# Retention followed by a gated feed-forward: one attention step moved and reordered, and three PSUM bank assignments changed

## Chip, cores, metric

The kernel runs on one core of a Trainium2 chip. The metric is the device time of one execution in microseconds (us). The span of a profiled execution, from its first to its last instruction, is shorter than the time reported for that same execution (308.8 against 310.72 for the kernel before); positions below count from the start of the span.

## Reference

```python
# attention without softmax: 8 batches, 8 heads, 576 positions, head dim 64
scores = q @ k.T / sqrt(64)
ret = scores * D          # D[h,i,j] = gamma_h ** (i-j) for i >= j, else 0
x = (ret @ v)             # -> (8*576, 512)
# feed-forward on 4608 tokens: w_in 512x2048, w_out 2048x512
h = x @ w_in
g = h * cos(h)
out = g @ w_out
```

All arrays are fp32 outside; the kernel multiplies in bf16.

## The kernel before

The engines go by the profile's names: TensorE (PE) multiplies matrices and writes to PSUM, a memory in banks from which VectorE (DVE) and ScalarE (ACT) read; GpSimd (POOL) prepares q, k and v; SyncE (SP) issues most of the DMAs, which load the inputs, store the output and, from group 8 on, transpose q and k into `qkT`.

Tokens are handled in 36 groups of 128. Attention of a group needs its scores (L173), a masked copy `ret` made by VectorE (L182), a running state (L201) and its masked copy `sb`, and an output (L230, L243) that is cast to `xT` (L255). The feed-forward takes tiles of 512, 256, 256 and then 512 tokens: `mm1` makes `h` in blocks of two PSUM banks (L270), ScalarE makes its cosine (L278), VectorE the product `gT` (L279), and `mm2` multiplies by w_out (L287). The order of all instructions is set by hand: attention steps of later groups are sown between the matmuls of earlier tiles.

PSUM has five tags, each with one buffer: `a`, `b`, `m` (two banks each), `n` and `st` (one each). A new use of a tag waits until the last reader of the old use has finished.

```python
def transposes(g, banks=None, only=(0, 1)):
    if g >= N_PE_T:                      # from group 8 on: by DMA
        nc.sync.dma_start(qkT, qks..., transpose=True)
        return
    for m in only:                       # groups below 8: on TensorE
        ps = psum.tile(..., tag=banks[m])
        ...                              # 4 transposes, then ScalarE copies ps to qkT

def scores(g, bank, idle=0):
    ps = psum.tile([P, 2, HG, P], F32, tag=bank)
    ...                                  # 8 matmuls qkT -> ps        (L173)
    nc.vector.tensor_tensor(out=ret, in0=ps, in1=mask)              # (L182)

def attn_out(gs, bank, evac=nc.vector.tensor_copy):
    ps = psum.tile([P, len(gs), HG, P], F32, tag=bank)
    ...                                  # sb x qT (L230), ret x vb (L243)
    evac(xT of these tokens, ps)                                    # (L255)

def mm1(n, et, c0, w, bank, inside={}):
    ps = psum.tile([P, 1024 // w, w], F32, tag=bank)
    for j in range(1024 // w):
        if j in inside: inside[j]()      # attention steps sown into a block
        ...                              # 4 matmuls                  (L270)
    # ScalarE: cos, VectorE: gT = ps * cos
# ... cut ...
banks = {0: "abmabmab", 1: "amba", 2: "bmab", 3: "mamabmab"}.get(n, "abmabmab")
inside = {
    (0, 0): {3: lambda: (state(3), attn_out([3], "m"))},
    (1, 0): {4: lambda: scores(5, "b")},
    (1, 1): {3: lambda: attn_out([5], "b", evac=nc.scalar.copy)},
}
# todo: (index of the mm2 matmul before which the step stands, step)
elif n == 2:
    todo = pair(g, "ab", 11, 24) + pair(g + 2, "ba", 31, 40)[:2]   # scores of 10 in b, of 11 in a
    late += [lambda: (state(g + 3), attn_out([g + 2, g + 3], "b"))]   # after block (3,1)
elif n + 1 < len(widths):
    todo = [ ...
        (25 if n == 3 else 20, lambda: (attn_out([g, g + 1], "m"), scores2(g + 2))),
        (52, lambda: (attn_out([g + 2, g + 3], "m"), scores2(g + 4))),   # in tile 3: scores of 16, 17
        ... ]
```

(The code is abridged; "..." stands for what is left out.) "Block (n,i)" below is block i of `mm1` in tile n, both counted from 0.

## Time and profile before

| | kernel before |
|---|---|
| time, first three runs | 312.71, 312.77, 312.76 us |
| span of the profiled execution | 308.8 us |
| TensorE (PE) busy | 302.1 us, 98% |
| TensorE weight loads | 171.2 us, 55% |
| VectorE (DVE), ScalarE (ACT) busy | 176.1 us, 116.7 us |

The page of the profile has the busy time by engine, and rows of 40 equal slices of the span (here 7.7 us each) in tenths:

```profile
PE 302.1 (98%) x2361; PEld 171.2 (55%) x2361; DVE 176.1 (57%) x179; ACT 116.7 (38%) x136; POOL 97.2 (31%) x120
...
PE   8899999999999999999999999999999999999996
...
DMA  8999999999999999999990999279935510110012
...
PE 72%; DMA 11%; SPq 11%; POOL 3%; issue 1%; ACT 1%; DVE 0%; POOLq 0%; ACTq 0%
```

PE is the bound. The last line is the chain of work that ended last: 72% of it is PE, but 22% of the span is DMA and the DMA-issuing queue (SPq). The DMA row says why: the 16 DMA engines are at 90% and more for the first half of the span.

A busy share of 98% does not say where PE waited, so its timeline is read at the places that the change touches. Columns: start, duration, engine, line, what, count, and in brackets the idle time before with what ended it. First PE from 17.5 to 22 us:

```profile
17.82 1.48 PE L270 MATMUL h<-xT,w_in_sb 128*128 128x256 bf16 x12
19.14 0.39 PE L201 MATMUL st<-vb,qks 128*128 128x128 bf16 x4
19.37 0.39 PE L230 MATMUL ov<-qT_112,sb 128*128 128x128 bf16 x4
19.68 0.41 PE L243 MATMUL ov<-ret,vb 128*64 128x128 bf16 x8
20.03 0.61 PE L270 MATMUL h<-xT,w_in_sb 128*128 128x256 bf16 x4
20.91 1.36 PE L270 MATMUL h<-xT,w_in_sb 128*128 128x256 bf16 x11 [0.27 <-DVE xT L255]
```

The same stretch on ScalarE:

```profile
18.09 0.62 ACT L158 CAST vb<-fv 128x512 bf16<-128x512 f32 x1 [1.33 <-DMA fv<-in_v_dram]
18.62 0.58 ACT L255 CAST xT<-ov 128x512 bf16<-128x512 f32 x1
```

Block (0,1) starts at 20.91, when the fourth group's `xT` is there. The ends of matmuls are modelled, so the idle time of 0.27 is too small: by starts (the distance between the starts of two matmuls, less the usual distance), the gap before it is 0.542 us where 0.109 is usual for 256 columns, a stall of 0.43.

Then PE around the start of the second tile, and from 84 to 88 us, and from 116.5 to 118.5 us:

```profile
49.28 0.38 PE L287 MATMUL o<-w_out_sb,gT 128*128 128x512 bf16 x1
49.73 1.05 PE L270 MATMUL h<-xT,w_in_sb 128*128 128x128 bf16 x16
...
84.08 0.62 PE L173 MATMUL sc<-qkT 64*128 64x128 bf16 x16
84.63 0.39 PE L287 MATMUL o<-w_out_sb,gT 128*128 128x512 bf16 x1
84.86 1.91 PE L270 MATMUL h<-xT,w_in_sb 128*128 128x256 bf16 x16
86.93 1.14 PE L270 MATMUL h<-xT,w_in_sb 128*128 128x256 bf16 x9 [0.16 <-DVE ret L182]
...
116.60 0.40 PE L173 MATMUL sc<-qkT 64*128 64x128 bf16 x8
117.30 0.40 PE L173 MATMUL sc<-qkT 64*128 64x128 bf16 x8 [0.31 <-DMA qkT<-qks]
```

From 49.28 to 49.73 are 0.446 us where a matmul of 512 columns takes 0.216: a stall of 0.23 that shows no bracket. At 86.93 PE waits for bank a (0.32 by starts), at 117.30 for the DMA that transposes qkT of group 17 (0.47 by starts).

### The profile page before, as it was taken

Reading aid. Unit: us, or ns where it says so; the run is one execution under the profiler, and the core shown is the slowest. Engines: PE = TensorE matmul, PEld = TensorE weight load, DVE = VectorE, ACT = ScalarE, POOL = GpSimd, SP = SyncE. Lnnn points to the kernel's source line nnn. Section 1 sums busy time; section 2 is a strip of 40 time slices with the busy share of each in tenths; the row PEclk is TensorE's granted clock in tenths of the full one; section 3 lists DMA queues with packets and bytes.
Section 4 is the critical chain, followed back from the end, with each engine's and each line's share of the span. In section 5 each row is a group of like instructions: output and inputs, shape, how many; then the busy total and the mean of one; then the engine's idle time right before and its main releaser. Section 6 shows DMA issues by size and latency. Waiting matters only on the chain.

```text
span 308.8 us, 5686 instructions
## 1 busy us (share of the span) xinstructions
PE 302.1 (98%) x2361; PEld 171.2 (55%) x2361; DVE 176.1 (57%) x179; ACT 116.7 (38%) x136; POOL 97.2 (31%) x120
## 2 busy tenths in 40 slices
PE   8899999999999999999999999999999999999996
PEld 3478547857588554445544554455445544554444
DVE  5766424565777764755466556755576556724610
ACT  3566234615046212640264016511551056015611
POOL 2740066644563554452542244214430000000000
PEclk9999999999999999999999999999999999999999
DMA  8999999999999999999990999279935510110012
GB/s 212 210 210 207 202 227 217 213 225 209 196 235 203 234 219 218 227 196 198 239 244 3 213 214 228 28 166 227 232 59 70 136 37 0 36 68 34 2 65 71
DMA packets 148697, 49.65 MB, mean 161 GB/s; under 512 B 138688, under 2 KB 144192, under 8 KB 148672
## 3 DMA queue, kind: packets, MB, share of 16 engines
q1 hardware_dynamic: 144448, 45.10, 77.3%
q0 software_dynamic: 4224, 4.19, 8.2%
q8 instruction: 18, 0.29, 0.4%
q14 instruction: 7, 0.06, 0.1%
HBM read 36.70 MB, written 9.44 MB: 149 GB/s over the span
## 4 chain that ended last, share of the span: by engine, by line
PE 72%; DMA 11%; SPq 11%; POOL 3%; issue 1%; ACT 1%; DVE 0%; POOLq 0%; ACTq 0%
PE o L287 33%; PE h L270 31%; SPq L107 8%; DMA fq<-in_q_dram 5%; DMA fk<-in_k_dram 5%; PE ov L243 2%; PE sc L173 2%; PE st L201 2%; SPq L146 2%; PE ov L230 1%; DMA qkT<-qks 1%; POOL qks L133 1%; POOL qks L132 1%; SPq L298 1%; PE tr L151 0%
## 5 line engine op out<-in xcount | busy, mean ns | idle before, releaser
L287 PE MATMUL o<-w_out_sb,gT 128*128 128x512 bf16 (+2 forms) x608 | 134.8, 368 | 0.3 <-DVE ret L182 0.3
L270 PE MATMUL h<-xT,w_in_sb 128*128 128x512 bf16 (+2 forms) x832 | 127.6, 313 | 0.6 <-DVE xT L255 0.3
L279 DVE TENSOR_TENSOR gT<-h,cosh 128x1024 bf16<-128x1024 f32 x72 | 88.2, 1225 | 56.7 <-ACT cosh L278 56.6
L270 PEld LDWEIGHTS <-w_in_sb 128*128 128x128 bf16 x832 | 75.7, 98 | 51.2 <-issue 1.5
L278 ACT ACTIVATE cosh<-h,half_pi 128x1024 f32<-128x1024 f32 x72 | 80.2, 1113 | 52.1 <-PE h L270 52.1
L287 PEld LDWEIGHTS <-gT 128*128 128x128 bf16 x608 | 55.3, 98 | 56.8 <-issue 0.6
L132 POOL TENSOR_TENSOR qks<-fq,gq 128x512 bf16<-128x512 f32 x32 | 33.3, 1042 | 107.9 <-DMA fq<-in_q_dram 103.0
L296 ACT COPY ot<-o 128x512 f32<-128x512 f32 (+2 forms) x38 | 21.4, 563 | 120.6 <-PE o L287 117.6
L133 POOL TENSOR_TENSOR qks<-fk,gk 128x512 bf16<-128x512 f32 x35 | 36.5, 1042 | 13.5 <-DMA fk<-in_k_dram 12.2
L182 DVE TENSOR_TENSOR ret<-sc,tri 128x1024 bf16<-128x1024 f32 x32 | 38.0, 1218 | 3.6 <-PE sc L173 3.6
L210 DVE TENSOR_TENSOR sb<-st,diag_105 128x512 bf16<-128x512 f32 x32 | 22.0, 687 | 28.9 <-PE st L201 28.9
L255 DVE CAST xT<-ov 128x1024 bf16<-128x1024 f32 (+1 forms) x17 | 19.7, 1161 | 24.3 <-PE ov L243 24.3
L139 POOL CAST vb<-fv 128x512 bf16<-128x512 f32 x32 | 19.5, 610 | 7.8 <-DMA fv<-in_v_dram 5.9
L201 PEld LDWEIGHTS <-qks 128*128 128x128 bf16 (+1 forms) x128 | 9.3, 97 | 7.5 <-issue 1.3
L201 PE MATMUL st<-vb,qks 128*128 128x128 bf16 (+1 forms) x128 | 12.4, 219 | 0.1
L243 PE MATMUL ov<-ret,vb 128*64 128x128 bf16 x288 | 12.0, 222 | 0.0
L173 PEld LDWEIGHTS <-qkT 64*128 64x128 bf16 x288 | 8.1, 94 | 5.8 <-ACT qkT L156 2.3
L173 PE MATMUL sc<-qkT 64*128 64x128 bf16 x256 | 10.3, 217 | 0.3 <-DMA qkT<-qks 0.3
L230 PEld LDWEIGHTS <-sb 128*128 128x128 bf16 x128 | 8.3, 98 | 3.7
L156 ACT COPY qkT<-tr 128x512 bf16<-128x512 bf16 x12 | 6.6, 587 | 9.0 <-PE tr L151 9.0
L243 PEld LDWEIGHTS <-vb 128*64 128x64 bf16 x288 | 8.7, 109 | 2.0
L230 PE MATMUL ov<-qkT,sb 128*128 128x128 bf16 (+1 forms) x116 | 8.8, 215 | 0.0
(45 smaller groups left out, 53.5 us busy)
## 6 DMA issues: line engine op xcount, KB each, us to landing
out_dram<-ot SPq DMA_DIRECT2D x35, 256.0 KB, 4.1
fk<-in_k_dram SPq DMA_DIRECT2D x32, 256.0 KB, 4.9
fv<-in_v_dram SPq DMA_DIRECT2D x32, 256.0 KB, 4.9
fq<-in_q_dram SPq DMA_DIRECT2D x28, 256.0 KB, 4.1
w_in_sb<-in_moe_w_in_dram POOLq DMA_DIRECT2D x4, 512.0 KB, 8.9
w_out_sb<-in_moe_w_out_dram POOLq DMA_DIRECT2D x4, 512.0 KB, 16.1
fq_110<-in_q_dram SPq DMA_DIRECT2D x2, 512.0 KB, 4.4
fq<-in_q_dram SPq DMA_DIRECT2D x8, 128.0 KB, 4.1
```

The lines of the kernel that those rows point to most:

```text
L107: i = nc.sync.dma_start(f[p0:p1], src[b, :, s0 : s0 + p1 - p0, :].rearrange("h s d -> s h d"))
L132: nc.gpsimd.tensor_tensor(out=qks[:, 0], in0=fq, in1=tq, op=ALU.mult)
L133: (nc.vector if g == 3 else nc.gpsimd).tensor_tensor(out=qks[:, 1], in0=fk, in1=tk, op=ALU.mult)
L173: nc.tensor.matmul(ps[:, he, hg, :], lhsT=qkT[d0 : d0 + D, HG + hg, :], rhs=qT[d0 : d0 + D, hg, :], start=True, stop=True,)
L182: nc.vector.tensor_tensor(out=ret.rearrange("p a b i -> p (a b) i"), in0=ps.rearrange("p a b i -> p (a b) i"), in1=mask.unsqueeze(1).to_br ...
L201: nc.tensor.matmul(ps[:, hg, :], lhsT=qks[p0:, 1, 2 * hg : 2 * hg + 2, :].rearrange("s h d -> s (h d)"), rhs=vb[p0:, 2 * hg : 2 * hg + 2, ...
L210: nc.vector.tensor_tensor(out=sb, in0=ps, in1=diag2.unsqueeze(1).to_broadcast([P, HG, P]), op=ALU.mult,)
L243: nc.tensor.matmul(ps[he * D : he * D + D, x, hg, :], lhsT=vb[:, 2 * hg + he, :], rhs=ret[:, he, hg, :], start=(g % PER == 0 and hg == 0), ...
L270: nc.tensor.matmul(ps[:, j, :], lhsT=w_in_sb[:, dg, (et + j) * P : (et + j + 1) * P], rhs=xT[:, dg, c0 : c0 + w], start=(dg == 0), stop=(d ...
L278: nc.scalar.activation(cosh, ps, ACTF.Sin, bias=half_pi, scale=1.0)
L279: nc.vector.tensor_mul(gT[:, et : et + m, c0 : c0 + w], ps, cosh)
L287: nc.tensor.matmul(ps, lhsT=gT[:, et, tsi * P : (tsi + 1) * P], rhs=w_out_sb[:, et, c0:c1], start=(et == 0), stop=(et == ET - 1),)
```

## The change

Its intent is to take PE's small stalls away. (1) The fourth group's output is issued before its state update and one step (4 matmuls) sooner, so that `xT` is ready when block (0,1) wants it. (2) Block (1,0) takes bank b instead of a, which ScalarE is still copying from. (3) To make room, scores and output of group 5 move to bank a; block (1,2) keeps b. (4) The scores of groups 10 and 11 swap banks, so that block (3,1), in a, follows the first `ret` and not the second. No instruction is added or removed.

```diff
-            vb = tiles.pop(("a", g))[1]
+            vb = tiles["a", g][1]
...
-        banks = {0: "abmabmab", 1: "amba", 2: "bmab", 3: "mamabmab"}.get(n, "abmabmab")
+        banks = {0: "abmabmab", 1: "bmba", 2: "bmab", 3: "mamabmab"}.get(n, "abmabmab")
...
-                (0, 0): {3: lambda: (state(3), attn_out([3], "m"))},
-                (1, 0): {4: lambda: scores(5, "b")},
-                (1, 1): {3: lambda: attn_out([5], "b", evac=nc.scalar.copy)},
+                (0, 0): {2: lambda: (attn_out([3], "m"), state(3))},
+                (1, 0): {4: lambda: scores(5, "a")},
+                (1, 1): {3: lambda: attn_out([5], "a", evac=nc.scalar.copy)},
...
-            todo = pair(g, "ab", 11, 24) + pair(g + 2, "ba", 31, 40)[:2]
+            todo = pair(g, "ab", 11, 24) + pair(g + 2, "ab", 31, 40)[:2]
```

(The first hunk only keeps the bookkeeping for a state update that now comes after the output.)

## The prediction

> **What bounds the kernel now.** The page gives TensorE (PE) 302.1 us busy of a 308.8 us span (98%); VectorE (DVE) 57%, ScalarE (ACT) 38%. The granted clock is full throughout. Matmul starts in the trace are 109 ns apart at 256 columns, 56 at 128, 216 at 512, as the Trainium skill says ("TensorE: Matmul & The Clock Gate", "Wait — 56ns, not 53.3ns?": N over 2.4 GHz plus about 2.5 ns). So the change, which adds and removes no instruction, can only win PE's stalls. Between the first tile and 120 us the matmul start times show five, as start gap minus normal gap:
> - 20.37 to 20.91: 0.43 us, block (0,1) waits for the fourth group's xT (DVE cast ends 20.86);
> - 49.28 to 49.73: 0.23 us, block (1,0) waits for bank a, which ACT still copies for the transposes (ends 49.67);
> - 86.93: 0.32 us, block (3,1) waits for bank a, held by the second mask multiply (ret);
> - 110.73: 0.44 us, a ret again, untouched;
> - 117.30: 0.47 us, scores wait for the DMA that transposes qkT.
> After 117.3 the waits by engine show none on PE.
>
> **What the change does, costed.**
> 1. Fourth group. Output goes first and after 8 instead of 12 matmuls, so at 18.71. But its bank m is freed only by ACT's xT cast of the third group (18.62 + 0.58 = 19.20), itself behind a vb cast that waited for its load until 18.09. PE will stall about 0.54 there. Then 0.66 us of output, 0.22 of state, 8 matmuls (0.87): block (0,1) starts at about 21.01 instead of 20.91; xT is ready by about 20.75. The xT stall goes, a bank stall comes: **+0.10 us**.
> 2. Block (1,0) in bank b: b's copy is the first of the two and done, stall gone: **-0.23**.
> 3. But block (1,2) is also in b, and now waits for gT of (1,0) (before: 53.29 + 1.23 = 54.52) while PE would be there 0.12 earlier than that: **+0.17**, a new stall near 54.4.
> 4. Scores of group 10 in a, of 11 in b: (3,1) needs only the first ret, done a DVE multiply (1.13) sooner: **-0.32**.
> Sum on PE by 87 us: about -0.28.
>
> **How much is critical.** Little. The chain of waits runs from 49.7 to 117.3 not over PE but over the DMA queue, the loads and GpSimd's preparation; DMA is at 90% and more in nearly all slices there. PE comes to 117.3 about 0.28 earlier and waits 0.75 instead of 0.47. The chain's root at 49.7 is an output copy on ACT that may come 0.10 later by step 1. So I expect -0.3 to +0.1, most likely near nothing.
>
> **Predicted: 312.70 us, 312.35 to 313.05 eight times in ten.** Faster by over 2%: 0.01; within 2%: 0.98; slower by over 2%: 0.01.
>
> **What will show it.** Right: the stall at 20.37 gone, one of about 0.5 at 18.7 released by the ACT cast; no gap at 49.7, block (1,0) about 0.13 earlier; a gap of 0.1 to 0.2 near 54.3; no gap at 86.9, block (3,1) about 0.28 earlier; the wait for qkT's DMA near 117.3 grown to about 0.75, and everything after within 0.1 of before. Wrong: that wait unchanged and all later work 0.3 earlier (then the loads follow PE).
>
> **What would make it wrong.** The load at 18.09 landing earlier (step 1 would then win 0.4); the DMA chain shifting by another order of transfers, by some tenths either way; a difference between sessions larger than these tenths.

## The result

The changed kernel took 312.07 us (median of 6, 311.63 to 313.75). The kernel before, in the rounds that alternated with it, took 312.16, 311.93 and 312.42; with its first three runs its median is 312.56. The ratio is 0.9996, 95% interval 0.9971 to 1.002: the same. A ratio here is the mean time of one kernel's fast runs over that of the other's, so it is not quite the ratio of the medians quoted. For this first comparison it takes in all six times of before; over the three alternating ones alone the means give 1.0005.

The page of the changed kernel:

```profile
PE 299.9 (97%) x2328; PEld 171.5 (55%) x2361; DVE 176.1 (57%) x179; ACT 116.8 (38%) x136; POOL 97.4 (31%) x120
...
PE   8899999999999998999999999999999999999996
...
DMA  8999999999999999999991899379935510110012
...
PE 89%; SPq 5%; DMA 4%; issue 1%; ACT 0%; DVE 0%; ACTq 0%
```

PE seems 2.2 us less busy, but this is not work saved: 2328 of the 2361 matmuls have a record, all weight loads are there. The span is 309.7 us. The chain's split between PE and DMA changed too: walked back from the end, it stays on PE from 109 us down to the start of the feed-forward instead of leaving for the DMA queue, though both kernels' chains pass through the same wait near 117 us, behind which the loads stand.

PE at the same places (17.5 to 22; 49 to 55; 84.05 to 87.9; 116.5 to 118.5 us):

```profile
17.80 1.05 PE L270 MATMUL h<-xT,w_in_sb 128*128 128x256 bf16 x8
19.21 0.38 PE L230 MATMUL ov<-qT_112,sb 128*128 128x128 bf16 x4 [0.37 <-ACT xT L255]
19.53 0.41 PE L243 MATMUL ov<-ret,vb 128*64 128x128 bf16 x8
19.87 0.40 PE L201 MATMUL st<-vb,qks 128*128 128x128 bf16 x4
20.11 2.13 PE L270 MATMUL h<-xT,w_in_sb 128*128 128x256 bf16 x18
...
49.57 1.06 PE L270 MATMUL h<-xT,w_in_sb 128*128 128x128 bf16 x16
...
84.11 0.82 PE L173 MATMUL sc<-qkT 64*128 64x128 bf16 x16
84.86 0.39 PE L287 MATMUL o<-w_out_sb,gT 128*128 128x512 bf16 x1
85.09 3.00 PE L270 MATMUL h<-xT,w_in_sb 128*128 128x256 bf16 x26
...
116.51 0.40 PE L173 MATMUL sc<-qkT 64*128 64x128 bf16 x8
118.21 0.40 PE L173 MATMUL sc<-qkT 64*128 64x128 bf16 x8 [1.31 <-DMA qkT<-qks]
```

The stall before block (0,1) is gone: the run of L270 from 20.11 has no break. In its place PE waits for ScalarE's cast before the output, at 19.21. The stall at 49.7 is gone as well, and so is the break in the L270 run at 86.9. But the 16 scores matmuls at 84.1 take 0.82 us instead of 0.62, and the wait for qkT's DMA near 117 has grown from 0.31 to 1.31 us.

To add this up, each weight load of the changed kernel was set against the same one of the first trace of before (the weight loads have no missing records, and the order differs only around 19 us). How much later the changed kernel is:

| at | changed minus before, us | step |
|---|---|---|
| 11 to 18 us | -0.03 | chance, ahead of the change |
| block (0,1), 20.9 | +0.08 | bank-m stall replaces xT stall: +0.10 |
| block (1,0), 49.7 | -0.15 | bank b free: -0.23 |
| inside block (1,2), 54.4 | +0.03 | new wait for gT of (1,0): +0.18 |
| scores of 11, 84.3 | +0.24 | new wait, not foreseen: +0.21 |
| block (3,1), 86.9 | -0.09 | no wait for the second ret: -0.33 |
| scores of 17, 117.3 | +0.91 | wait for the DMA of qkT: +1.00 |
| last matmul | +0.91 | nothing more |

(The new wait of step 3 shows in the matmul starts as one gap of 0.225 us, from 54.200 to 54.425, where 0.056 is usual.) So nearly all that differs in the end arises at one wait. From 117.3 us on PE runs the last 190 us in lockstep with before.

The chain view (start, duration, what) shows the transfer behind that wait, before and then changed:

```profile
113.04 4.22 DMA qkT<-qks
...
113.53 4.64 DMA qkT<-qks
```

It was issued 0.49 us later, a lag that the queue already had at the transpose of group 11 (79.85 against 79.36), and it took 0.42 us longer. The 0.91 us must not be read as the cost of the change, though: it is the distance between two single executions, 311.63 and 310.72 us. That of before was faster than all six of its timed runs (311.93 to 312.77), and the medians do not show such a loss.

### The profile page after: what moved, and what is told of

It is laid out like the page before. It is cut to its first block, busy times and chain, and to the rows that moved or that the text cites. A ratio compares the mean times of both kernels' runs of the same rounds, so it can differ in the third digit from the quotient of the medians.

```text
span 309.7 us, 5653 instructions
## 1 busy us (share of the span) xinstructions
PE 299.9 (97%) x2328; PEld 171.5 (55%) x2361; DVE 176.1 (57%) x179; ACT 116.8 (38%) x136; POOL 97.4 (31%) x120
## 4 chain that ended last, share of the span: by engine, by line
PE 89%; SPq 5%; DMA 4%; issue 1%; ACT 0%; DVE 0%; ACTq 0%
PE h L270 40%; PE o L287 38%; SPq L107 3%; PE ov L243 3%; PE sc L173 3%; DMA fv<-in_v_dram 2%; PE st L201 2%; PE ov L230 2%; DMA qkT<-qks 1%; PE tr L151 1%; SPq L146 0%; DVE xT L255 0%; SPq L298 0%; SPq L325 0%; ACT vb L158 0%
## 5 line engine op out<-in xcount | busy, mean ns | idle before, releaser
L287 PE MATMUL o<-w_out_sb,gT 128*128 128x512 bf16 (+2 forms) x583 | 131.1, 368 | 2.6 <-issue 1.6
L270 PE MATMUL h<-xT,w_in_sb 128*128 128x512 bf16 (+2 forms) x826 | 127.1, 313 | 0.5
L270 PEld LDWEIGHTS <-w_in_sb 128*128 128x128 bf16 x832 | 75.9, 98 | 50.2 <-issue 0.4
```

The source lines that it names most:

```text
L270: nc.tensor.matmul(ps[:, j, :], lhsT=w_in_sb[:, dg, (et + j) * P : (et + j + 1) * P], rhs=xT[:, dg, c0 : c0 + w], start=(dg == 0), stop=(d ...
L287: nc.tensor.matmul(ps, lhsT=gT[:, et, tsi * P : (tsi + 1) * P], rhs=w_out_sb[:, et, c0:c1], start=(et == 0), stop=(et == ET - 1),)
```

## The experiments

Theory A, from the prediction: PE meets the DMA chain of the loads at the scores of group 17, and what happens before it on PE is absorbed there. Such a place, where PE cannot go on before a DMA has landed, is called a gate below; it is opened by moving the step that needs the data to a later place. The rivals: B, that wait is no gate, and the chain comes back elsewhere; C, the change itself delayed the DMA chain; D, what PE wins earlier counts in full. Twelve kernels ran. Every one was correct, and "before" is the kernel before in the same rounds on the same chip: the three sessions of experiments fell on three chips, and the median of before was 312.56 in the first comparison and 311.31, 311.50 and 311.08 us in these, a spread as large as the largest effect here.

| kernel | what it is | median (lowest to highest), us | before, us | ratio (95%) |
|---|---|---|---|---|
| b_late | gate at 17 open | 310.57 (310.29 to 313.57) | 311.31 (310.99 to 313.68) | 0.9977 (0.9939 to 1.0014) |
| a_late | change + gate at 17 open | 310.66 (310.17 to 316.74) | same | 0.9963 (0.9934 to 0.9993) |
| mend | change, new stalls mended | 311.31 (310.57 to 311.76) | same | 0.9984 (0.9953 to 1.0014) |
| mend_late | mend + gate at 17 open | 310.56 (309.93 to 311.87) | same | 0.9970 (0.9938 to 1.0001) |
| b_again | none | 311.13 (one run) | 311.50 (310.78 to 313.48) | |
| p3_gates | bank swap of 10/11, both gates open | 312.08 (311.60 to 315.28) | same | 1.0016 (0.9982 to 1.005) |
| a_gates | change, both gates open | 311.74 (311.69 to 311.91) | same | 1.0002 (0.9976 to 1.0029) |
| mend_gates | mend, both gates open | 310.99 (310.91 to 312.97) | same | 0.9988 (0.9956 to 1.002) |
| p3_gates2 | as p3_gates, own stall removed | 310.35 (310.25 to 310.37) | 311.08 (310.38 to 312.06) | 0.9976 (0.9960 to 0.9991) |
| a_gates2 | as a_gates, likewise | 310.38 (310.27 to 310.47) | same | 0.9977 (0.9962 to 0.9993) |
| mend_gates2 | as mend_gates, likewise | 309.82 (309.63 to 311.04) | same | 0.9968 (0.9948 to 0.9987) |
| mend_all | mend_gates2 + one more stall removed | 309.49 (309.27 to 310.85) | same | 0.9954 (0.9935 to 0.9973) |

The only run named slow is a_late's 316.74, at a granted clock of 0.989; it is in no ratio. The differences discussed are under 1%, and rest on the traces first and on the times where their spread allows.

### b_late and a_late: open the gate at group 17

```diff
-                (52, lambda: (attn_out([g + 2, g + 3], "m"), scores2(g + 4))),
+                (52, lambda: (attn_out([g + 2, g + 3], "m"), scores(g + 4, "a") if n == 3 else scores2(g + 4))),
+                (62 if n == 3 else 53, lambda: scores(g + 5, "b") if n == 3 else None),
```

b_late is before with this edit, a_late is the changed kernel with it.

> The kernel before, with the scores of group 17 alone moved 10 matmuls of 512 columns (10 x 0.216 = 2.16 us) later, past the wait for the DMA that transposes its qkT. Theory A (that wait is the gate: everything before it on PE is absorbed, and its landing time, which varies from execution to execution, sets the total): no wait for qkT's DMA left on PE, time about 0.5 to 0.9 us below before (0.2 to 0.3%), and a smaller spread of the single times than before's 0.8 us. Rival B (the wait is not a gate; the DMA chain comes back at the next scores or in the next tile): same time as before within 0.1 us, the wait seen elsewhere.

> The changed kernel with the same move. Theory A: with the gate gone, what the change did to PE must show: its trace reached the third wide tile 0.09 us ahead of before (-0.26 if scores of group 11 do not wait for their own DMA there), so 0.1 to 0.3 us below b_late, and 0.5 to 1.2 us below before. Rival B: as before within 0.1 us. Rival C (the change itself delayed the DMA chain by the 0.9 us that its trace shows at 117 us): a wait for a qkT DMA remains in a_late, and b_late is faster than a_late.

In both, the median fell by about 0.7 us, and no wait is left at group 17. Rival B in its strong form (no gain) falls, by the traces, which show no such wait after it, and by a_late's interval; b_late's still includes 1, and one run of 313.57 spoils the smaller spread that was expected of it. But a_late is not below b_late, and both traces have a wait for a qkT DMA at another place, 0.4 and 0.3 us at the scores of group 11. PE, from 84.05 to 87.9 us in a_late:

```profile
84.12 0.40 PE L173 MATMUL sc<-qkT 64*128 64x128 bf16 x8
84.84 0.40 PE L173 MATMUL sc<-qkT 64*128 64x128 bf16 x8 [0.32 <-DMA qkT<-qks]
```

This is the unforeseen stall of the changed kernel's table above, larger here. There are two gates, not one. By its letter the test for rival C is met (a wait remains, b_late is faster), but b_late has the same wait, and longer, so it does not speak for C.

### mend and mend_late: make PE's lead larger

```diff
-        banks = {0: "abmabmab", 1: "bmba", ...
+        banks = {0: "abmabmab", 1: "bmab", ...
-                (0, 0): {2: lambda: (attn_out([3], "m"), state(3))},
+                (0, 0): {2: lambda: (attn_out([3], "n"), state(3))},
-            todo = [(4, lambda: transposes(6, "mb")), (9, lambda: transposes(7, "mb"))]
+            todo = [(4, lambda: transposes(6, "ma")), (9, lambda: transposes(7, "ma"))]
```

(against the changed kernel; mend_late also has the edit of a_late)

> The changed kernel with both new stalls of the change mended: the fourth group's output goes to the one-bank tag n instead of m (no wait for the third group's cast), and the second tile's four blocks take banks b, m, a, b instead of b, m, b, a (the third block no longer waits for the first one's gT); transposes 6 and 7 go to m and a. Scores of 17 stay where they were. On PE: -0.43 at 20.9 us, -0.23 at 49.7, -0.32 at 86.9, about -1.0 us in all against before ahead of the wait. Theory A: absorbed, the wait for qkT near 117 grows to 1.4 us or more and the time is that of before within 0.3 us. Rival D (what PE wins there counts in full): 1.0 us below before.

> The mended kernel with scores of 17 moved. Theory A: -1.0 us of PE stalls and -0.5 to -0.9 of the gate both count: 1.3 to 1.9 us below before (0.4 to 0.6%), 0.7 to 1.0 below b_late; unless the 2.16 us of slack is used up by PE's lead, when part of the wait returns. Rival B or D alone: not below mend.

Both mends did what they were for. Against the first trace of before, mend is 0.13 us ahead by chance before the change begins, 0.56 ahead at block (0,1) and 0.79 at block (1,0), so it won 0.43 and 0.23 there, and the lead holds past block (1,2) up to 84 us; so the bank-m stall of step 1 and the gT wait of step 3 are shown to be what the changed kernel lost there. And yet mend's median equals that of before to the hundredth, 311.31. Its trace shows where the lead went, from 84.05 and from 116.5 us:

```profile
84.50 0.40 PE L173 MATMUL sc<-qkT 64*128 64x128 bf16 x8 [0.81 <-DMA qkT<-qks]
...
117.94 0.40 PE L173 MATMUL sc<-qkT 64*128 64x128 bf16 x8 [1.07 <-DMA qkT<-qks]
```

Much of the lead is lost at group 11, where the expectation did not look. Rival D falls by this trace; the interval of the times (0.9953 to 1.0014) would still allow its 1.0 us. The expectation for mend_late was missed: it is no faster than b_late. In its trace one gate took all:

```profile
85.96 0.40 PE L173 MATMUL sc<-qkT 64*128 64x128 bf16 x8 [2.17 <-DMA qkT<-qks]
```

With the gate at 17 open, PE's lead was absorbed at the gate at 11, in this execution. It is one of the two slowest of the six (311.77 us, where four lie between 309.93 and 310.73), so it shows that the gate can take all, not that it usually does.

### b_again: the kernel before, traced a second time

> The kernel before, unchanged, for a second trace. Theory A2 (PE meets the DMA chain at two gates, the scores of group 11 at 84.3 us and those of group 17 at 117.3, whose landing times vary by about a microsecond between executions of one and the same kernel): PE starts agree with the first trace within 0.05 us up to 84 us, and differ by 0.2 to 1.5 us after one of the two gates. Rival C (the changes moved the DMA chain): both gates where the first trace has them, within 0.1 us.

PE is a constant 0.08 us earlier than in the first trace from 11 to 84 us (the expectation said 0.05), then meets both gates (84.05 to 87.9 us, and 116.5 to 118.5 us):

```profile
84.58 0.40 PE L173 MATMUL sc<-qkT 64*128 64x128 bf16 x8 [0.19 <-DMA qkT<-qks]
84.91 0.39 PE L287 MATMUL o<-w_out_sb,gT 128*128 128x512 bf16 x1
85.14 3.00 PE L270 MATMUL h<-xT,w_in_sb 128*128 128x256 bf16 x26
...
117.70 0.40 PE L173 MATMUL sc<-qkT 64*128 64x128 bf16 x8 [0.74 <-DMA qkT<-qks]
```

The unchanged kernel has the wait at 84.5 too, and the gate at 17 opens at 117.70 instead of 117.30; its last matmul comes 0.39 us later than in the first trace. So landing times vary between executions of one kernel, by an amount as large as what the change could win. (The two traces may come from different chips; no chip is recorded for the first. But times of before spread as widely within one session on one chip.) Of the 0.91 us in the changed kernel's trace, 0.39 were therefore also seen without the change.

Whether the rest is chance or the change's doing (rival C) two traces of before cannot say, but every packed trace holds the landing, also where PE did not wait for it. These are the traces without and with steps 1 to 3 (p3_gates, where a load came 3.5 us late, and the mended kernels left out):

| qkT landed at, us | before, b_again, b_late, p3_gates2 | changed, a_late, a_gates, a_gates2 |
|---|---|---|
| group 11 | 84.25, 84.53, 84.92, 84.51 | 84.49, 84.80, 84.29, 84.38 |
| group 17 | 117.26, 117.65, 117.65, 117.42 | 118.17, 117.81, 117.86, 117.58 |

In the two pairs that share a session and differ by the change alone (b_late and a_late; p3_gates2 and a_gates2, by steps 1 to 3 of it), the change comes with a landing 0.12 and 0.13 us earlier at group 11, and 0.16 later in both at group 17. A delay of 0.9 us by the change is in no other pair; one of 0.2 us at group 17 these traces cannot exclude. The time from issue to landing at group 17 is 4.08 to 4.24 us in all traces but the changed kernel's (4.64): what varies is mostly when the queue comes to issue it. Why the queue drifts stays open.

There is a second lesson in the line at 85.14: its L270 run has no break at 86.9. The second `ret` frees bank a at a time set by VectorE; when PE comes 0.2 to 0.3 us late out of the gate at 11, it no longer waits there. Step 4 removes a stall of 0.32 us only in executions in which the gate at 11 does not hold PE up by as much.

### p3_gates, a_gates, mend_gates: open both gates, first try

```diff
-            todo = pair(g, "ab", 11, 24) + pair(g + 2, "ab", 31, 40)[:2]
+            todo = pair(g, "ab", 11, 24) + [
+                (26, lambda: state(g + 2)), (31, lambda: scores(g + 2, "a"))]
...
             mm1(n, et, c0, cw, banks[i], inside)
+            if (n, i) == (3, 0):
+                scores(11, "b")
```

plus the edit for group 17. p3_gates is before with step 4 alone and these edits (step 4 is needed, or block (3,1) would wait for the delayed scores); the others start from the changed and the mended kernel.

> The kernel before with only the third part of the change (scores of group 10 in a, of 11 in b), and with both gates opened: the scores of 11 after the first block of the third tile (1.75 us later), those of 17 ten matmuls later (2.16 us). Theory A2: no wait for a qkT DMA on PE; the trace is 0.32 + 0.47 = about 0.8 us shorter than the first trace of before, and the single times spread by less than 0.3 us apart from slow ones. If the gates are not the cause of the spread: spread as before, about 1 us.

> The changed kernel with both gates opened. Theory A2: with nothing to absorb it, parts 1 and 2 of the change show as they do in the traces, +0.07 (or +0.09), -0.22, +0.22: 0.05 to 0.1 us slower than p3_gates in the trace, and the times within 0.2 us of p3_gates.

> The mended kernel (no new bank waits) with both gates opened. Theory A2: 0.43 + 0.22 = about 0.65 us below p3_gates and 0.7 below a_gates, in the trace and in the times: 0.4 to 0.5% below before. If PE's lead of 0.65 us uses up the slack, part of it returns as a wait at one of the gates, then seen in the trace.

No wait for a qkT DMA is left on PE in any of the three traces, and a_gates's six times lie within 0.22 us, where before spread over 2.7 in the same rounds. They are 0.34 below p3_gates's, not within 0.2 as expected, because that kernel had high runs (below). mend_gates is 0.75 us below a_gates, as expected: with the gates open, PE's lead counts. But nothing became faster than before, because the edit brought a stall of its own. PE in mend_gates from 84 to 91 us:

```profile
87.84 0.39 PE L201 MATMUL st<-vb,qks 128*128 128x128 bf16 x4
89.41 0.61 PE L230 MATMUL ov<-qkT,sb 128*128 128x128 bf16 x8 [1.19 <-DVE ret L182]
```

VectorE's timeline in the same stretch says why:

```profile
87.00 1.22 DVE L279 TENSOR_TENSOR gT<-h,cosh 128x1024 bf16<-128x1024 f32 x1 [1.99 <-ACT cosh L278]
88.14 1.21 DVE L182 TENSOR_TENSOR ret<-sc,tri 128x1024 bf16<-128x1024 f32 x1
```

The mask of group 11 now stood behind the product `gT` of block (3,0), which waits for the cosine. That was a mistake of the experiment, and p3_gates's expected gain of 0.8 us was missed for it. Also, p3_gates's median is raised by three high runs; its profiled one (315.28 us) shows a cause that has nothing to do with the gates, a load of w_in that came late (17 to 22 us):

```profile
19.74 2.53 PE L270 MATMUL h<-xT,w_in_sb 128*128 128x256 bf16 x11 [1.61 <-DMA w_in_sb<-in_moe_w_in_dram]
```

### p3_gates2, a_gates2, mend_gates2, mend_all: open both gates, mended

```diff
+                (3, 0): {3: lambda: scores(11, "b")},        # inside block (3,0), instead of after it
```

and for mend_all also

```diff
-                (25 if n == 3 else 20, lambda: (attn_out([g, g + 1], "m"), scores2(g + 2))),
+                (22 if n == 3 else 20, lambda: (attn_out([g, g + 1], "m"), scores2(g + 2))),
```

> As p3_gates, but the scores of group 11 stand inside the first block of the third tile (after 12 of its 16 matmuls), so that VectorE masks them ahead of that block's multiply. That takes away the stall of 1.35 us that the three gates kernels brought (output of groups 10 and 11 waiting for a ret queued behind gT). Theory A2: 1.3 us below p3_gates's usual 311.65, so about 310.3; no wait for a qkT DMA; the usual times within 0.3 us of each other, with rare ones 1 to 4 us higher where a load of w_in comes late, as in the trace of p3_gates.

> The changed kernel with both gates opened this way. Theory A2: 0.05 to 0.1 us above p3_gates2 (parts 1 and 2 of the change cost +0.07, -0.22, +0.22 on PE); about 310.4, 1.3 us below a_gates.

> The mended kernel with both gates opened this way. Theory A2: 0.75 us below a_gates2 as mend_gates was below a_gates (about 309.65), 0.5% below before; if PE's lead uses up the slack at a gate, a wait for qkT's DMA of up to 0.5 us returns in the trace and the spread with it.

> mend_gates2, and in the third tile the step that outputs groups 12 and 13 and scores 14 and 15 comes 3 matmuls of 512 columns sooner (0.65 us), so that the accumulation in bank a at 110.7 us does not wait for the mask of 14: 0.44 us below mend_gates2, about 309.2, unless the qkT of group 15 has not landed by then (the DMA chain a third time).

The waits of PE in p3_gates2 (total, times, longest, in us) no longer name qkT's DMA:

```profile
PE idle L164 <- DVE zeros L345: 1.3, 1, 1.3
PE tr L151 <- POOL qks L133: 0.6, 2, 0.4
PE o L287 <- DVE ret L182: 0.3, 1, 0.3
PE h L270 <- DVE xT L255: 0.3, 1, 0.3
PE sc L173 <- ACT qkT L156: 0.2, 1, 0.2
```

p3_gates2's five times lie between 310.25 and 310.37, a_gates2's between 310.27 and 310.47; before spread from 310.38 to 312.06 in the same rounds. In all five runs each, both kernels thus ran at the lowest time that before reached, so the gates make at least part of the spread of before. They are not all of it: with the gates open other kernels still had single high runs (p3_gates up to 315.28, mend_gates 312.97, mend_gates2 311.04, mend_all 310.85 us). The trace of p3_gates2 ends 0.38 us ahead of the first trace of before. That is less than the 0.79 us of waits removed (0.32 and 0.47), because two extra breaks of the matmul stream have a price: block (3,1) is 0.11 ahead where 0.32 were removed, and behind the scores of 17 another 0.27 ahead where 0.47 were removed, about 0.2 us for each break. The starts show it directly: at 83.76 us the step from a 512-column matmul into the scores takes 312 ns where 216 is usual, and at 84.26 the step out of them 148 ns where 53 is usual; the break inside block (3,0) costs the same (205 ns where 109 is usual, and 148 again).

a_gates2 against p3_gates2 is the cleanest reading of steps 1 to 3: 310.38 against 310.35 us, and in the traces, taken against the offset of 0.08 us that the two have before the change begins, +0.08 at block (0,1), -0.14 at (1,0), +0.04 at (1,2) and +0.03 at the end. They are worth nothing together. mend_gates2 against p3_gates2, as the traces stand (0.03 apart before the change begins): -0.41, -0.63, -0.63, and 309.82 against 310.35 us; it is 0.56 below a_gates2 where 0.75 was expected. mend_all wins another 0.44 us in its trace after 106 us, as expected (0.33 in the medians), and is the fastest: 309.49 us where about 309.2 was expected, 0.5% below before, ratio 0.9954 with an interval that excludes 1. The changed kernel was not run in these rounds. Step 4 alone with the gates open was not compared to a kernel without it.

## Why the prediction was right or wrong

- **The time**: "same" (0.98) was right: the ratio of 0.9996 times the 312.76 us that the prediction started from is 312.63. But the changed kernel's plain median, 312.07, lies 0.28 below the stated range. Before read lower too in those rounds (312.17 on average), and 1.1 to 1.5 us lower in the experiments' sessions. The range was drawn from three runs that happened to agree within 0.06 us, so that the ratio falls inside it is partly luck. The prediction did name both dangers, a shift of the DMA chain and a difference between sessions.
- **Step 1, +0.10**: right. The stall at bank m came as described (start gap 0.644 where 0.109 is usual, so 0.54 us, as predicted), and block (0,1) lost 0.10 us in the changed kernel's trace, 0.08 in a_gates2's.
- **Step 2, -0.23**: right, -0.23.
- **Step 3, +0.17**: right, +0.18. mend, with another order of banks, has neither this loss nor that of step 1.
- **Step 4, -0.32**: the stall went, -0.33. But 0.21 us in front of it came at the scores of group 11, and an unchanged kernel that waits there (b_again) does not have this stall at all.
- **"Sum on PE by 87 us: about -0.28"**: wrong, -0.06 when the 0.03 us of chance is taken off. The term that failed is one missing from the sum: the landing of qkT for group 11, +0.21 in this trace, and waits from 0.19 to 2.17 us in five traces of the experiments. The first trace of before has no wait there, and the prediction does not name the place. It had no slack: qkT landed at 84.25 us and the first weight load that needs it began at 84.29, 0.04 us later, as in every trace that does wait there.
- **"PE comes to 117.3 about 0.28 earlier and waits 0.75 instead of 0.47"**: right that this wait absorbs PE's lead (mend shows it, with two waits of 1.88 us and no gain in time), wrong in size: 1.47 by starts (the gap of 0.524 became 1.523).
- **"Everything after within 0.1 of before"**: wrong for this trace, +0.91. The landing was taken as a constant of the kernel; it varies between executions, +0.39 in the unchanged kernel's second trace. Whether the change adds some 0.2 us to it is open.
- **"How much is critical. Little."**: right, and shown both ways: with the gates closed a lead of 0.66 us on PE gave nothing (mend against before), with them open it gave 0.75 us (mend_gates against a_gates).

## What to carry to other kernels

When the chain of waits runs through loads for part of the span, a stall removed before the next point where compute needs a load is worth nothing until that point is given slack; find all such points, also those which show no wait in the one trace at hand, because a zero wait can mean no slack at all, as at group 11 here. Tracing the unchanged kernel twice shows which waits are fixed and which are chance, and how wide a predicted range must be. When a PSUM bank is exchanged to dodge one reader, list the next user of the bank taken as well: here 0.18 of the 0.23 us gained was paid back some five microseconds later.

## What the Trainium skill lacked or had wrong

- "TensorE: Matmul & The Clock Gate", "Back-to-back issue gap": it gives a stream of weight-load and matmul pairs about 131 ns per matmul of 512 columns and about 81 ns at 128, and calls N/2.4 + 2.5 the isolated gap. In this kernel, where every matmul has its weight load, the steady start-to-start distances are 216 ns at 512, 109 at 256 and 56 at 128, so the formula holds in the stream and those two figures do not.
- "TensorE: Matmul & The Clock Gate": no page gives the time that a stream of full-array matmuls loses when half-array ones are sown in; moving 8 scores matmuls out of a run of 16 into a run of their own cost about 0.2 us on PE, in each of two places.
- "PSUM — Partial Sum Buffer", "PSUM bank collisions raise a hardware error" says to guard PSUM with semaphores by bank and quadrant, or more simply by bank; it does not say what a release costs. In the trace of before the waiting matmul starts about 0.05 us after the end of what it waits for (49.67 to 49.73 for bank a; 20.86 to 20.91 for `xT`, which is not in PSUM).
- No page that was consulted says how much the landing of a DMA transpose behind a queue of loads varies between executions of one kernel: here 117.26 and 117.65 us for the same transfer, 4.22 us after its issue both times.
